# Grouped-query attention and a gated MLP on one core: scores of eight units taken in pairs, and two loads per batch moved

## The chip, the cores and the metric

The kernel runs on one core of one Trainium2 chip. The metric is device time in microseconds (us), the median of several runs, lower is better. The core's engines work side by side: TensorE (PE, matmuls and transposes, its weight loads shown as PEld), VectorE (DVE), ScalarE (ACT), GpSimd (POOL) and SyncE (SP, which here only issues DMAs). They meet through semaphores.

## The reference

Two stages, in a row, for 8 batches of 384 rows:

```python
# attention: q [8,16,384,64], k and v [8,4,384,64]; 4 query heads share one k/v head
scores = (1 / np.sqrt(D)) * np.matmul(q, k.transpose(0, 1, 3, 2))
attn = softmax(scores)                       # over the last axis
x = np.matmul(attn, v) -> [8, 384, 1024]     # the 16 heads side by side
# gated MLP with a spatial gate
h = np.maximum(x @ w_in, 0.0)                # w_in [1024, 1024]
u, v = h[..., :512], h[..., 512:]
v_n = (v - mean(v)) / np.sqrt(var(v) + 1e-06)
v_s = einsum('ts,bsd->btd', w_spatial, v_n) + b_spatial[None, :, None]
out = (u * v_s) @ w_out                      # w_out [512, 1024], float32
```

## The kernel before

**Units.** The attention of a batch is cut into 18 units, counted on through the batches, so that unit 18 is the first of batch one and unit 144 would be the end. Three units (three blocks of 128 keys) make a set: 128 query positions of eight query heads. A batch has six sets; sets 0 and 1 cover the first 128 query positions, and so on. For a unit, `units` (L264 to L287) issues two score matmuls `sc` (L278): each contracts over 64 rows, the two use the two halves of TensorE's rows, and each writes a PSUM bank of 128 x 512. `exp` (L288) has ACT turn each into `aT`. When a set's exps are there, `weigh` (L292) multiplies `aT` by v in 12 matmuls `av` per row half (L298), and DVE divides by the sums: a reciprocal `r` (L311) and a product `x` (L313).

**From x to the MLP.** The MLP wants x transposed (`xt`). In batch zero PE does it (`x_turn`, L324, tile `xps`, copied by DVE at L216). From batch one on a DMA does (`x_send`, L334, issued by SP at L337), one for each 128 query positions, when both of their sets are weighed. q and k are transposed likewise: by PE for the first two batches (`q_turn`, `k_turn`; tiles `qps`, `kps`, copied to `qT`, `kT` by DVE), later by DMA (`q_send`, `k_send`, L256 and L248). The MLP's parts on PE are `pv` (L353, x times the second half of w_in), `pu` (L412, the first half), `psp` (L431, the spatial gate) and `po` (L469, w_out); each ends in an eviction by DVE or ACT: `vr` (L367) with statistics (L379, L380), `uT` (L423), `vs` (L443), `osb` (L216). POOL normalizes (`vn`, L397) and gates (`gT`, L448).

**The order on PE** is written out. A loop over units 0 to 20 (`ALONE = 21`) issues the scores of one unit, then the steps due at that unit (`todo`: transposes, casts, loads), then the weighings due, and then pours matmuls of the MLP, drawn from the generator `gated`, until a budget `spare` is used up: 736 ns for a unit, less 224 for each transpose and 372 for each weighing. From unit 21 on a second loop takes three units (a whole set) at a time: six scores in a row, then fractions of a fixed share of MLP matmuls between the weighings and the due steps.

**PSUM** has eight banks. `bank` gives each new tile the bank that by a planner's estimated release times comes free first; the release times come from fixed costs in `reads`. If the estimate is off, PE waits for the engine that empties the bank.

**Loads.** For batches four to seven a loop (L674 ff.) sets, by units ahead of the batch's first unit `u0`, when loads, casts (POOL) and transposing sends are issued. Loads of k, v and q, the sends and the stores of finished rows all go through SP's one queue in program order, so an instruction that waits there holds back those behind it. `at` appends to the list of a unit; within a group of three units the second loop issues the steps of all three together, behind the late weighings and so behind `x_send`.

Of the kernel before, what the change touches and what calls it, by code (L numbers as in the profile page):

```python
# [17 lines left out]
def kernel(  # L18
# [58 lines left out]
    def bank(shape, dtype, name):  # L77
        i = min(range(8), key=done.__getitem__)
        t = ps.tile(shape, dtype, name=name, tag=f"bank{i}")
        clock[nc.tensor] = max(clock[nc.tensor], done[i])  # L80
        done[i] = 1e12 + clock[nc.tensor]
        taken[name] = i
        return t

    def spend(ns):
        clock[nc.tensor] += ns

    def reads(eng, ns, name=None):
        clock[eng] = max(clock[eng], clock[nc.tensor] + 200.0) + ns
        if name:  # L90
            done[taken.pop(name)] = clock[eng]
# [172 lines left out]
    def units(u, count):  # L264
        b, r = divmod(u, UNITS)
        s, kt0 = divmod(r, NT)
        qt, j = divmod(s, 2)
        kts = range(kt0, kt0 + count)
        if kt0 == 0:
            aTs[b, s] = att.tile([P, NT, 2, G * P], FP16, name=f"aT_{b}_{s}", tag="aT", bufs=3)  # L270
        scs = [
            (kt, hh, bank([P, G * P], FP32, f"sc_{b}_{s}_{hh}_{kt}"))
            for hh in range(2)
            for kt in kts
        ]
        for kt, hh, sc in sorted(scs, key=lambda x: x[:2]):
            rows = slice(hh * D, (hh + 1) * D)
            nc.tensor.matmul(  # L278
                sc,
                kTs[b][rows, j, kt * P : (kt + 1) * P],  # L280
                qTs[b, j][rows, qt].rearrange("p (r i c) -> p i r c", r=G, i=G),
                start=True,
                stop=True,
            )
        spend(count * C512 + 186)
        return [(aTs[b, s][:, kt, hh], sc, f"sc_{b}_{s}_{hh}_{kt}") for kt, hh, sc in scs]

    def exp(a, sc, name):  # L288
        reads(act, 480.0, name)
        act.activation(a, sc, AF.Exp, scale=scale)  # L290

    def weigh(b, s, hh):  # L292
        qt, j = divmod(s, 2)
        aT = aTs[b, s]
        av = bank([P, 512], FP32, f"av_{b}_{s}_{hh}")
        for kt in range(NT):
            for i in range(G):
                nc.tensor.matmul(  # L298
                    av[:, i * (D + 1) : (i + 1) * (D + 1)],
                    aT[:, kt, hh, i * P : (i + 1) * P],  # L300
                    v1[b % 2][:, 2 * j + hh, kt, 0 : D + 1],
                    start=(kt == 0 and i == 0),
                    stop=(kt == NT - 1 and i == G - 1),
                )
        if s == 0 and hh == 0:
            x16s[b] = att.tile([P, NT, DM], FP16, name=f"x16_{b}", tag="x16")
        o = av[:, 0 : G * (D + 1)].rearrange("p (i d) -> p i d", i=G)
        spend(372)
        r = small.tile([P, G, 1], FP32, name=f"r_{b}_{s}_{hh}", tag="r")
        reads(dve, 600.0, f"av_{b}_{s}_{hh}")  # L310
        dve.reciprocal(r, o[:, :, D : D + 1])  # L311
        c = j * 512 + hh * 256
        dve.tensor_tensor(  # L313
            x16s[b][:, qt, c : c + 256].rearrange("p (i d) -> p i d", i=G),
            o[:, :, 0:D],
            r.to_broadcast([P, G, D]),
            ALU.mult,
        )
        measure()
# [243 lines left out]
    def at(n, f, *args):  # L563
        todo.setdefault(n, []).append((f, args))
# [109 lines left out]
    for b in range(4, B):  # L674
        u0 = UNITS * b
        at(u0 - 24, load_k, b)
        at(u0 - 24, load_v, b)
        at(u0 - 22, load_q, b, 0)
        at(u0 - 20, load_q, b, 1)
        at(u0 - 16, cast_k, b, pool)  # L680
        at(u0 - 14, cast_q, b, 0, pool)
        at(u0 - 12, k_send, b)
        at(u0 - 10, q_send, b, 0)
        at(u0 - 10, cast_q, b, 1, pool)
        at(u0 - 8, q_send, b, 1)
        at(u0 - 4, cast_v, b, pool)
# [9 lines left out]
    def pour(n, owed):  # L696
        while owed > 0:
            if n < wait_for[0]:
                return 0.0
            x = next(fill, None)  # L700
            if x is None:
                return 0.0
            if isinstance(x, tuple):
                wait_for[0] = x[1]
            else:
                owed -= x
        return owed

    def turn_x(b, s, n):
        if s % 2 and b:  # L710
            x_send(b, s // 2)

    ALONE = 21
    F = (0.2, 0.3, 0.1, 0.4)
    owed = 0.0
    halves = {}
    for u in range(ALONE):
        for pair in units(u, 1):
            exp(*pair)
        spare = 736  # L720
        for f, args in todo.pop(u, []):
            f(*args)
            spare -= 224 if f in (q_turn, x_turn, k_turn) else 0
        for b, s in ends.pop(u, []):
            halves.setdefault(u, []).append((b, s, 0))
            halves.setdefault(u + (0 if s == 0 else 1), []).append((b, s, 1))
        for h in halves.pop(u, []):
            weigh(*h)
            spare -= 372
            if h[2]:  # L730
                turn_x(*h[:2], u)
        owed = pour(u, min(owed, 0) + spare)
# [64 lines left out]
```

## Time and profile before

| | us |
|---|---|
| median of 3 runs | 239.31 (238.87 to 239.68) |
| the profiled execution, its own time | 239.07 |
| its span, first to last instruction | 237.0 |
| PE busy | 230.4 |
| ACT busy | 169.4 |
| DVE busy | 142.9 |
| POOL busy | 101.4 |

The span is what the profile's times count in; the 2.07 us around it belong to the launch. Ends of matmuls are modelled in the profile, so for PE the differences between starts tell more than durations. Lines named L... are lines of the kernel before. The page's groups show the matmuls of scores with 380 ns each, but two of them run side by side. The waits view lists idle time of an engine over 0.15 us and what ended it; shorter waits of PE are seen only in the time line.

### The profile page before, as it was taken

The page shows a single profiled execution, that of the slowest core. Times are in us where ns is not written, and L with a number is a line of the kernel's source. Part 1 is how long each engine was busy: PE and PEld are TensorE (multiplying, and loading weights), DVE is VectorE, ACT ScalarE, POOL GpSimd, SP SyncE. Part 2 cuts the span into 40 slices and gives each one's busy share as a digit, 9 for nine tenths or more (in the row PEclk, how much of TensorE's full clock was granted, in tenths as well). Part 3 has the DMA queues.
Part 4 walks back from the last instruction along what each step waited for, and adds up shares of the span by engine and source line. Part 5 has one row for each costly group of instructions (what it writes and reads, how often), then busy time and mean ns, then how long its engine had stood idle before and what let it go on. Part 6 is the DMA issues. An engine that isn't in the chain of part 4 may idle for free.

```text
span 237.0 us, 5921 instructions
## 1 busy us (share of the span) xinstructions
PE 230.4 (97%) x2312; PEld 123.3 (52%) x2312; DVE 142.9 (60%) x379; ACT 169.4 (71%) x348; POOL 101.4 (43%) x145
## 2 busy tenths in 40 slices
PE   6999999999999999999999999999999999999993
PEld 6545565645554445555464445555465455545541
DVE  2668775676447674566645577366744767367362
ACT  2999989969897869978697776986597776401211
POOL 3679583551466442275045800566022500460550
PEclk9999999999999999999999999999999999999999
DMA  6999949999999999997998599929912543240147
GB/s 184 290 321 313 278 116 166 167 321 215 297 226 238 332 300 180 354 205 184 169 309 203 182 207 295 272 88 159 253 27 44 114 147 96 48 177 0 66 200 268
DMA packets 67467, 47.47 MB, mean 200 GB/s; under 512 B 48336, under 2 KB 60416, under 8 KB 67440
## 3 DMA queue, kind: packets, MB, share of 16 engines
q1 hardware_dynamic: 62512, 39.86, 67.7%
q0 software_dynamic: 3952, 6.42, 12.1%
q10 hardware_dynamic: 976, 0.82, 1.1%
q8 instruction: 18, 0.29, 0.5%
q14 instruction: 9, 0.07, 0.1%
HBM read 25.95 MB, written 12.58 MB: 163 GB/s over the span
## 4 chain that ended last, share of the span: by engine, by line
PE 79%; DMA 15%; DVE 1%; POOL 1%; SPq 1%; issue 0%
PE pu L412 17%; PE po L469 16%; PE pv L353 15%; PE sc L278 12%; PE av L298 12%; PE psp L431 6%; DMA xt<-x 4%; DMA w_in<-in_moe_w_in_dram 4%; DMA q<-in_q_dram 3%; DMA v_None<-in_v_dram 2%; DMA qT<-q 2%; POOL vn L397 1%; PE qps L238 1%; DVE osb L216 1%; POOL q L204 0%; SPq L256 0%
## 5 line engine op out<-in xcount | busy, mean ns | idle before, releaser
L290 ACT ACTIVATE aT<-sc 128x512 f16<-128x512 f32 x288 | 147.7, 618 | 31.5 <-PE sc L278 30.5
L298 PEld LDWEIGHTS <-aT 128*128 128x128 f16 x1152 | 47.0, 97 | 16.8 <-issue 2.0
L353 PE MATMUL pv<-w_in,xt 128*128 128x512 f16 x192 | 50.9, 380 | 0.4 <-DMA w_in<-in_moe_w_in_dram 0.2
L298 PE MATMUL av<-v,aT 128*128 128x65 f16 x1152 | 50.5, 193 | 0.0
L469 PE MATMUL po<-w_out,gT 128*128 128x512 f16 (+2 forms) x196 | 50.5, 375 | 0.0
L412 PE MATMUL pu<-xt,w_in 128*128 128x384 f16 x256 | 49.9, 326 | 0.0
L397 POOL TENSOR_SCALAR vn<-vr,rstd,nmr 128x512 f16<-128x512 f32 x23 | 17.7, 783 | 69.9 <-DVE nmr L392 48.5
L448 POOL TENSOR_TENSOR gT<-vs,uT 128x384 f16<-128x384 f32 x31 | 32.5, 1059 | 31.9 <-DVE r L311 16.9
L313 DVE TENSOR_TENSOR x<-av,r 128x256 f16<-128x256 f32 x96 | 40.7, 424 | 3.3
L278 PE MATMUL sc<-qT,kT 64*128 64x512 f16 x288 | 42.3, 380 | 0.5 <-DVE qT L216 0.2
L311 DVE RECIPROCAL r<-av 128x4 f32<-128x4 f32 x96 | 17.1, 178 | 40.8 <-PE av L298 40.5
L216 DVE COPY osb<-po 128x512 f32<-128x512 f32 (+1 forms) x39 | 26.6, 683 | 17.3 <-PE po L469 17.2
L412 PEld LDWEIGHTS <-w_in 128*128 128x128 f16 x256 | 22.1, 98 | 17.1 <-issue 5.5
L423 ACT ACTIVATE uT<-pu 128x384 f16<-128x384 f32 x32 | 15.8, 495 | 16.1 <-PE pu L412 16.0
L469 PEld LDWEIGHTS <-gT 128*128 128x128 f16 x196 | 17.4, 98 | 17.3 <-issue 3.3
L353 PEld LDWEIGHTS <-xt 128*128 128x128 f16 x192 | 15.8, 97 | 18.0 <-issue 5.1
L278 PEld LDWEIGHTS <-kT 64*128 64x128 f16 x288 | 11.0, 94 | 25.4 <-issue 13.8
L431 PE MATMUL psp<-wsT,vn 128*128 128x384 f16 x96 | 22.2, 327 | 0.0
L443 DVE TENSOR_TENSOR vs<-psp,bias_bc 128x384 f32<-128x384 f32 x32 | 17.6, 552 | 7.0 <-PE psp L431 6.9
L367 DVE TENSOR_SCALAR vr<-pv 128x512 f32<-128x512 f32 x24 | 16.4, 682 | 8.4 <-PE pv L353 8.3
L201 POOL CAST q<-q 128x768 f16<-128x768 f32 x22 | 17.7, 833 | 7.8 <-PE av L298 3.0
L379 DVE BATCH_NORM_STATS2 stats<-vr 128x6 f32<-128x512 f32 x24 | 16.4, 685 | 0.1
(47 smaller groups left out, 98.0 us busy)
## 6 DMA issues: line engine op xcount, KB each, us to landing
out_dram<-osb SPq DMA_DIRECT2D x21, 512.0 KB, 2.8
q<-in_q_dram SPq DMA_DIRECT2D x10, 768.0 KB, 7.3
v_None<-in_v_dram SPq DMA_DIRECT2D x6, 384.0 KB, 4.5
w_in<-in_moe_w_in_dram POOLq DMA_DIRECT2D x4, 512.0 KB, 10.4
k_None<-in_k_dram SPq DMA_DIRECT2D x5, 384.0 KB, 3.9
q<-in_q_dram POOLq DMA_DIRECT2D x2, 768.0 KB, 8.7
out_dram<-osb SPq DMA_DIRECT2D x5, 256.0 KB, 2.3
w_out<-in_moe_w_out_dram POOLq DMA_DIRECT2D x2, 512.0 KB, 9.4
```

The lines of the kernel that those rows point to most:

```text
L201: eng.tensor_copy(t16[:, :, :, hh, :], src[:, hh])
L216: (act.copy if eng is act else dve.tensor_copy)(o, i)
L278: nc.tensor.matmul(sc, kTs[b][rows, j, kt * P : (kt + 1) * P], qTs[b, j][rows, qt].rearrange("p (r i c) -> p i r c", r=G, i=G), start=True ...
L290: act.activation(a, sc, AF.Exp, scale=scale)
L298: nc.tensor.matmul(av[:, i * (D + 1) : (i + 1) * (D + 1)], aT[:, kt, hh, i * P : (i + 1) * P], v1[b % 2][:, 2 * j + hh, kt, 0 : D + 1], st ...
L313: dve.tensor_tensor(x16s[b][:, qt, c : c + 256].rearrange("p (i d) -> p i d", i=G), o[:, :, 0:D], r.to_broadcast([P, G, D]), ALU.mult,)
L353: nc.tensor.matmul(pv, xts[b][:, kt, st * P : (st + 1) * P], w_in16[:, kt, DH:DFF], start=(kt == 0), stop=(kt == NK - 1),)
L397: (dve if b == 0 and st == 1 else pool).tensor_scalar(vn, v_r.pop((b, st)), rstd[:, st : st + 1], nmr[:, st : st + 1], op0=ALU.mult, op1=A ...
L412: nc.tensor.matmul(pu[:, 0:S], w_in16[:, kt, m * P : (m + 1) * P], xts[b][:, kt, :], start=(kt == 0), stop=(kt == NK - 1),)
L431: nc.tensor.matmul(psp[:, 0:S], v_n[b, st][:, m * P : (m + 1) * P], wsT16[:, st, :], start=(st == 0), stop=(st == NT - 1),)
L448: pool.tensor_tensor(gT, vs, uT, ALU.mult)
L469: nc.tensor.matmul(po[:, 0:width], gTs[b][:, m, tt * P : (tt + 1) * P], w_out16[:, m, c0 : c0 + width], start=(m == 0), stop=(m == NM - 1),)
```

## The change

Units 13 to 20 are taken two at a time: at units 13, 15, 17 and 19 the loop issues the scores and exps of that unit and the next, and at 14, 16, 18 and 20 none. The steps and weighings due at each unit stay with it. The budget for MLP matmuls becomes 600 ns at the units with scores and 870 at those without.

For batches four to seven the second q load moves from 20 to 17 units ahead of the batch, and the v load from 24 to 15 units ahead. In the loop of three units at a time this puts the q load behind the last `x_send` of the batch two in front, and the v load one group of three later.

```diff
@@ -674,9 +674,9 @@
     for b in range(4, B):
         u0 = UNITS * b
         at(u0 - 24, load_k, b)
-        at(u0 - 24, load_v, b)
         at(u0 - 22, load_q, b, 0)
-        at(u0 - 20, load_q, b, 1)
+        at(u0 - 17, load_q, b, 1)
+        at(u0 - 15, load_v, b)
         at(u0 - 16, cast_k, b, pool)
         at(u0 - 14, cast_q, b, 0, pool)
         at(u0 - 12, k_send, b)
@@ -714,10 +714,15 @@
     F = (0.2, 0.3, 0.1, 0.4)
     owed = 0.0
     halves = {}
+    TWO = 13
     for u in range(ALONE):
-        for pair in units(u, 1):
-            exp(*pair)
-        spare = 736
+        if u < TWO or (u - TWO) % 2 == 0:
+            pairs = units(u, 1)
+            if u >= TWO and u + 1 < ALONE:
+                pairs += units(u + 1, 1)
+            for pair in pairs:
+                exp(*pair)
+        spare = 736 if u < TWO else (600 if (u - TWO) % 2 == 0 else 870)
         for f, args in todo.pop(u, []):
             f(*args)
             spare -= 224 if f in (q_turn, x_turn, k_turn) else 0
```

## The prediction

> **What bounds the kernel now.** I read the page's first part (busy time by engine), then the waits, then the time line of PE around the edited units, DVE's beside it, and last the chain that ended last, at its DMA links.
>
> ```profile
> PE 230.4 (97%) x2312; PEld 123.3 (52%) x2312; DVE 142.9 (60%) x379; ACT 169.4 (71%) x348; POOL 101.4 (43%) x145
> ```
>
> PE is busy for 97% of the span, at a granted clock of 0.998. So time is won only by taking work or a short wait out of PE's stream; what another engine saves counts only where PE waits for it. The edited units run between 17 and 32 us; that stretch, and under it PE's rows of it, with a group of three units from later in the run:
>
> ```profile
> 17.00:32.00 15.00, 14.93 (x206) 8.33 (x205) 11.82 (x37) 13.87 (x28) 11.06 (x20) 1.00 1.02 278
> ```
>
> ```profile
> 17.24 0.59 PE L353 MATMUL pv<-w_in,xt 128*128 128x512 f16 x2
> 17.77 0.39 PE L278 MATMUL sc<-qT,kT 64*128 64x512 f16 x2
> ...
> 18.86 0.39 PE L278 MATMUL sc<-qT,kT 64*128 64x512 f16 x2
> 19.18 0.54 PE L298 MATMUL av<-v,aT 128*128 128x65 f16 x12
> ...
> 72.03 0.82 PE L278 MATMUL sc<-qT,kT 64*128 64x512 f16 x6
> 72.78 0.60 PE L469 MATMUL po<-w_out,gT 128*128 128x512 f16 x2
> ```
>
> The columns of the first are PE, PEld, DVE, ACT, POOL (us busy of 15.00): PE 14.93, ACT 13.87, DVE 11.82. All three are nearly full here, unlike in the whole span. Of the time line read the differences between starts. A pair of scores (x2, the two row halves run side by side) holds PE from 18.86 to 19.18, 0.32 us; two pv ahead of one hold it from 17.24 to 17.77, 0.53, where two of them inside a run take 0.43. So one unit alone costs 0.10 + 0.32 = 0.42 us. Three units together go from 72.03 to 72.78: 0.75, with the 0.10 ahead 0.85, so a further unit in the same group costs (0.85 - 0.42) / 2 = 0.21. A score group thus pays about 0.20 us for being a group.
>
> DVE, which empties most of PSUM, in the same stretch:
>
> ```profile
> 20.34 0.68 DVE L379 BATCH_NORM_STATS2 stats<-vr 128x6 f32<-128x512 f32 x1
> 21.06 0.18 DVE L380 BATCH_NORM_AGGREGATE mv<-stats 128x2 f32<-128x6 f32 x1
> 21.16 0.15 DVE L311 RECIPROCAL r<-av 128x4 f32<-128x4 f32 x1
> 21.34 0.42 DVE L313 TENSOR_TENSOR x<-av,r 128x256 f16<-128x256 f32 x1
> ...
> 31.05 0.41 DVE L216 COPY qT<-qps 128x512 f16<-128x512 f16 x1
> 31.38 0.42 DVE L216 COPY xt<-xps 128x512 f16<-128x512 f16 x1
> ```
>
> The x of 21.34 ends at 21.77; PE's x turn that reads it starts at 21.81. The xt copy ends at 31.80, and the fourth score of the group at 31.19, whose bank it frees, starts at 31.85 (0.43 behind the third; 0.01 is usual). So PE's next losses lie on DVE.
>
> From the chain, the links where PE meets a DMA after the start:
>
> ```profile
> 50.15 4.90 DMA qT<-q
> 55.09 1.15 PE sc L278 x6
> ...
> 75.15 10.13 DMA xt<-x
> 85.33 0.60 PE pv L353 x2
> ```
>
> These two landings (at 55.05 and 85.28) are met by PE without slack: whatever PE gains before them is lost there unless the landing comes earlier too.
>
> **Edit 1, scores two units in a row.** The instructions stay the same; the order on PE changes. Of the eight groups of two scores of units 13 to 20, four go into the group before them: 4 x 0.20 = 0.81 us less on PE (0.203 unrounded). This is on the path, as PE has no idle time to hide it in. The pours change from 8 x 736 = 5888 ns to 4 x (600 + 870) = 5880: the matmuls that fill PE between scores are the same, except that one pv (0.215) goes ahead of unit 21 instead of behind it. From unit 24 on the order on PE is the old one.
>
> What it adds is pressure on DVE and on the banks. The DVE instructions are the same and in the same order, so I walked them beside PE from unit 13 (18.86) on, with the steps of the rows: av to its end 0.54 and 0.04 to the next engine, r to x 0.21, x to the next 0.34, a copy 0.33, vr 0.60, stats 0.72, mv 0.10. Six places where PE then waits:
>
> - x turn of x columns 4 to 7 behind units 15 and 16: PE is there at 21.81 as before, but the first av of set 3 now stands behind four scores and ends at 19.94 instead of 19.72, so r starts 19.98, x 20.20, stats 20.54, r 21.36, x 21.56 to 21.98. PE waits 0.19, where it waited 0.
> - the pv and the x turn behind the next two pairs, each for an xt or x just copied: 0.05 and 0.05.
> - the group of units 21 to 23: its second score takes the bank of the last pv, whose copy vr runs from 26.99 to 27.67: 0.14 lost (before 0.10: start 27.87, end 28.72, against 0.75).
> - x turn of the last set of batch one: its bank is that of the av before, whose x ends 30.10; PE is there at 29.85: 0.29 (before the av behind it lost 0.08).
> - the group of units 24 to 26: its fourth score waits for the xt copy, by the walk to 31.32 (before 31.80): 0.31 lost there. Before 0.43 there and 0.09 ahead of it.
>
> New waits 0.19 + 0.05 + 0.05 + 0.14 + 0.29 + 0.31 = 1.03, old ones 0.10 + 0.08 + 0.09 + 0.43 = 0.70. So 0.33 of the 0.81 is given back and 0.48 stays: pv behind unit 26 at 31.89 instead of 32.37. Bounds: 0.81 if DVE's waits are no longer than before (and 0.70 more could in principle go with them, though DVE's own 11.82 of 15.00 us leave little), 0 if DVE's chain sets the pace. I take the walk, as its steps are rows of this very stretch.
>
> ACT: an exp follows the one before at 0.49 us, four take 1.95; two units in the walk take 2.1 to 2.3 on PE, so ACT waits 0.15 to 0.3 per pair and does not bind. The nearest bank that an exp must free for a score (unit 18's, by the exp of unit 16) is free 0.3 us ahead.
>
> A rule that speaks against edit 1: the Trainium skill, TensorEngine Tiling (Array Packing), Performance Considerations, says that tiling makes TensorE faster but not the emptying of PSUM, which may become the bottleneck. By that rule taken fully edit 1 would bring nothing and the time be 238.9. The trace agrees in part: the 31.80 to 31.85 handover is such a wait, and DVE still has 3.18 us free.
>
> At 55.09 the lead of 0.48 meets the qT landing. Without that landing PE would have started those scores at 54.94; but the fourth of them starts at 55.65, when vr has emptied its bank, and the pv behind at 56.29, when x (55.72 + 0.42) has emptied another. These follow PE and come 0.48 earlier. Were the landing not to move at all, scores from 55.09 would give the pv at 55.83 to 55.85, which still keeps 0.44 to 0.46. And it should move: its chain goes back through q loads and sends in SP's order to the x send at 34.26, released by an x of DVE at 34.23, which comes earlier with PE. Later landings have more slack: qT of batch three 70.97 for scores at 72.03, q of batch two's second set 58.33 for 59.65.
>
> **Edit 2, the loads.** On SP's queue, for batch four, k, v, q0, q1, out, x send become k, q0, out, x send, q1, out, v, x send of batch three. The x send of 75.15 takes 10.13 us: ahead of it 384 + 384 + 768 + 768 + 512 KB stand in the same queue, landing at 76.2, 77.3, 80.5, 83.1 and 84.5, then xt at 85.28. Without v (1.15 us) and q1 (2.56) it lands near 85.28 - 3.71 = 81.6. PE wants it at 85.18 (84.43 + 0.75), so 0.14 of waiting goes and, more to the point, the lead of edit 1 survives: it would need the landing at 84.7. SP issues nothing more or less, and no load gains a wait of length: the buffers of q1 and v have been read 20 us earlier. What moves behind: q1 lands near 84 to 85 (before 83.1), v near 87, behind the next out (before 77.3). POOL casts q1 at 83.20 and v at 84.75 now, and next has vn at 93.25; so POOL waits some 2 us longer and has 6 us to spare. Ahead of the x send of batch three (82.90) SP's queue holds the same transfers as before in another order, so that send and kT and qT behind it should land as now: qT of batch four at 92.58 and 94.00, wanted at 96.70 and 100.78. In batches five to seven PE has no wait for a DMA now (no PE idle over 0.15 us from 80 to 200), and x sends have 5 us and more, so there the edit is worth 0.
>
> **Sum**, against the profiled execution's own 239.07 (span 237.0 and 2.07 around it): -0.81 + 0.33 - 0.14 = -0.62, so 238.45. That execution is 0.24 below the median 239.31 and inside the runs (238.87 to 239.68).
>
> **The rivals.**
> 1. The waits on DVE do not grow: the whole 0.81 + 0.14 comes, 238.1. For it: the six waits are each under 0.3 us and built from handovers of 0.04; against it: DVE has 3.2 us free in 15, in pieces.
> 2. The lead is lost, to a chain on DVE that sets the pace or to transfers that keep their times: 0.14 is left, 239.07 - 0.14 = 238.9. For it: DVE is at 79% of that stretch (11.82 of 15.00); against: the walk.
> 3. Slower: scores four in a row want four banks at once. If the second unit's scores find theirs still to be read by an exp, PE stands for one exp (0.49) in each of the four pairs, 1.95, against the 0.81 saved: 239.07 + 1.95 - 0.81 - 0.14 = 240.1. It decides from about 0.24 us per pair on. The walk has 0.3 us of slack there, so exps would have to come 0.5 us later than their rows.
> 4. Slower by the loads: v or q1 of batch four lands so late that POOL's vn starts behind 93.25, or qT after 96.70. From there each us late costs a us; it takes 4 to 6 us more than worked out above. I count it with rival 3.
>
> **Chances and range.** Forecast 0.46, rival 1 0.24, rival 2 0.16, rivals 3 and 4 0.14. The forecast's own range is 238.2 to 238.75 (0.25 either way, the sum of six waits of 0.05 to 0.3). For 8 in 10: down to rival 1 less the part of old waits that might go, 237.8, and up past rival 2 to 239.4, which leaves out most of rivals 3 and 4. From no change one can tell about 0.3%, 0.72 us: below 238.35 lie rival 1 and a third of the forecast, 0.40; within it the rest of it and rival 2, 0.46; slower 0.14.
>
> **What would show it.** PE's score groups of x4 at about 18.9, 21.1, 23.2 and 25.3 us; pv behind unit 26 near 31.9; DVE as what ends PE's short waits at 22.0, 27.7, 30.1 and 31.4; xt of batch two landing near 82 and PE's scores near 84 without the wait behind. Wrong would be: exps as releaser of scores in that stretch, the lead at 56 us smaller than at 32, or a POOL or PE wait on q, v or qT of batch four.

## The result, and the profile after

The changed kernel's median is 238.94 us over 21 runs (237.84 to 239.68). The kernel before, run beside it and with the three first runs counted in, had 240.65 over 21 (238.53 to 244.4). The ratio is of the fast runs alone: it leaves out three of before (242.53 to 244.4 us, more than 1.5% above its fastest), and the other 18 have a median of 239.68, 0.74 us above the changed kernel's. It is 0.9952, with a 95% interval of 0.993 to 0.9973: faster by half a percent, where the likeliest case of the prediction was a gain of 0.26%, inside the 0.3% that one can tell from no change. The profiled execution took 238.38 us with a span of 236.4 (before 239.07 and 237.0); the prediction's sum was 238.45.

The first part of the page of the changed kernel, and its stretch from 17 to 32 us (columns PE, PEld, DVE, ACT, POOL in us busy):

```profile
PE 230.1 (97%) x2312; PEld 123.6 (52%) x2312; DVE 142.7 (60%) x379; ACT 169.5 (72%) x348; POOL 101.5 (43%) x145
```

```profile
17.00:32.00 15.00, 14.85 (x210) 8.66 (x209) 12.39 (x38) 14.25 (x29) 12.32 (x23) 1.00 1.04 287
```

The shares over the span say nothing of the change. In the stretch the same 15 us hold more work: ACT 14.25 for 13.87, DVE 12.39 for 11.82. PE's time line of the pairs, start and duration ahead:

```profile
18.98 0.61 PE L278 MATMUL sc<-qT,kT 64*128 64x512 f16 x4
19.52 0.54 PE L298 MATMUL av<-v,aT 128*128 128x65 f16 x12
...
21.22 0.61 PE L278 MATMUL sc<-qT,kT 64*128 64x512 f16 x4
21.76 0.34 PE L224 MATMUL kps<-ident,k 128*128 128x128 f16 x3
21.93 0.49 PE L330 MATMUL xps<-ident,x 128*128 128x128 f16 x4
22.26 0.39 PE L238 MATMUL qps<-ident,q 128*128 128x128 f16 x4
22.48 0.53 PE L298 MATMUL av<-v,aT 128*128 128x65 f16 x12
22.94 0.39 PE L353 MATMUL pv<-w_in,xt 128*128 128x512 f16 x1
23.27 0.60 PE L278 MATMUL sc<-qT,kT 64*128 64x512 f16 x4
...
25.32 0.61 PE L278 MATMUL sc<-qT,kT 64*128 64x512 f16 x4
...
29.63 0.39 PE L238 MATMUL qps<-ident,q 128*128 128x128 f16 x4
30.17 0.40 PE L330 MATMUL xps<-ident,x 128*128 128x128 f16 x4
...
30.86 1.10 PE L278 MATMUL sc<-qT,kT 64*128 64x512 f16 x6
31.89 0.82 PE L353 MATMUL pv<-w_in,xt 128*128 128x512 f16 x3
```

Two units go from 18.98 to 19.52, 0.54 us, with 0.10 ahead 0.64, against 2 x 0.42 before: the 0.20 per group is there. The four groups start within 0.12 us of the places predicted (18.9, 21.1, 23.2, 25.3). The x turn of 21.93 to 22.26 takes 0.33 instead of 0.23: a wait for x of 0.10, which the prediction put at 0.19. Other waits are read in the same way. The av of 22.48 is followed by a pv after 0.46 us, where 0.37 is usual, because the pv reads an xt copied just before (0.09). From qps at 29.63 to xps at 30.17 it is 0.54 instead of 0.22, a wait for the bank of an av, whose x ends at 30.11 (0.31). The six scores of 30.86 take 1.03 instead of 0.75 (0.28), and those of unit 21, at 27.56, take 0.90 (0.14). The pv behind unit 26 starts at 31.89, the time predicted, though this execution reached unit 13 0.12 us later than that of before.

At the landing of xt of batch two, SP's queue and then PE in the changed kernel, and last PE in the kernel before:

```profile
71.95 0.53 SPq L112 DMA_DIRECT2D k_None<-in_k_dram  x1
72.53 0.54 SPq L122 DMA_DIRECT2D q<-in_q_dram  x1
73.18 0.41 SPq L484 DMA_DIRECT2D out_dram<-osb  x1
74.18 1.99 SPq L337 DMA_TRANSPOSE xt<-x  x1
```

```profile
83.92 0.82 PE L278 MATMUL sc<-qT,kT 64*128 64x512 f16 x6
84.68 0.60 PE L353 MATMUL pv<-w_in,xt 128*128 128x512 f16 x2
```

```profile
84.43 0.82 PE L278 MATMUL sc<-qT,kT 64*128 64x512 f16 x6
85.33 0.60 PE L353 MATMUL pv<-w_in,xt 128*128 128x512 f16 x2
```

The x send is issued at 74.18 and its data land 8.3 us later, at 82.46 (before: issued 75.15, landed 85.28). The scores of 83.92 are followed after 0.76 us by the pv that reads xt, where before it was 0.90: the 0.14 us of waiting are gone.

What can't be seen in one pair of traces is how much of the difference is the edits'. So for every traced execution I took the starts of PE's scores and read the run in stretches. Unit n to unit m means from the first score of n to the first score of m.

| execution | unit 11 starts | unit 13 | 13 to 27 | 63 to 66 | 66 to the end | xt of batch two landed | span |
|---|---|---|---|---|---|---|---|
| before | 16.55 | 18.86 | 17.06 | 4.10 | 148.46 | 85.28 | 237.00 |
| changed | 16.67 | 18.98 | 16.46 | 3.97 | 148.47 | 82.46 | 236.36 |

The executions of the experiments are added below. From unit 66 on all agree to 0.05 us. Before unit 13, which neither edit reaches, the changed kernel's execution was 0.12 us later than that of before, so behind the start the two differ by 0.64 + 0.12 = 0.76 us: 0.60 between units 13 and 27, 0.13 at the landing, 0.04 between units 36 and 39. The last belongs to that one execution of before: in two others, traced later, before took the same 4.18 us there as the changed kernel.

### The profile page after: what moved, and what is told of

The parts are those of the page before. It is cut to its first block, busy times and chain, and to the rows that moved or that the text cites. A ratio compares the mean times of both kernels' runs of the same rounds, so it can differ in the third digit from the quotient of the medians.

```text
span 236.4 us, 5917 instructions
## 1 busy us (share of the span) xinstructions
PE 230.1 (97%) x2312; PEld 123.6 (52%) x2312; DVE 142.7 (60%) x379; ACT 169.5 (72%) x348; POOL 101.5 (43%) x145
## 4 chain that ended last, share of the span: by engine, by line
PE 93%; DVE 2%; DMA 2%; issue 0%; ACTq 0%; ACT 0%
PE pu L412 18%; PE pv L353 18%; PE po L469 18%; PE sc L278 15%; PE av L298 15%; PE psp L431 7%; DMA q<-in_q_dram 2%; PE qps L238 1%; PE xps L330 1%; DVE x L313 1%; DVE osb L216 1%; DVE qT L216 0%; DVE q L206 0%; DVE r L311 0%; DVE vr L367 0%
## 5 line engine op out<-in xcount | busy, mean ns | idle before, releaser
L278 PE MATMUL sc<-qT,kT 64*128 64x512 f16 x288 | 41.6, 380 | 0.4 <-DVE qT L216 0.2
L278 PEld LDWEIGHTS <-kT 64*128 64x128 f16 x288 | 10.9, 94 | 23.7 <-issue 12.1
```

The lines of the kernel that those rows point to most:

```text
L278: nc.tensor.matmul(sc, kTs[b][rows, j, kt * P : (kt + 1) * P], qTs[b, j][rows, qt].rearrange("p (r i c) -> p i r c", r=G, i=G), start=True ...
```

## The experiments

My theory after the result: the gain is 0.60 us of PE time from the pairs, kept by the earlier landing; what the medians show beyond that is scatter of the start. The rivals: the landing moves by itself and the loads need not be moved; or the loads are the main thing, as they spare executions with late transfers; or DVE sets the pace and more grouping would bring nothing.

**Each edit alone, both again, and before against itself.** The first kernel has only the pairs:

```diff
-        at(u0 - 17, load_q, b, 1)
-        at(u0 - 15, load_v, b)
+        at(u0 - 24, load_v, b)
+        at(u0 - 20, load_q, b, 1)
```

> Only the scores of units 13 to 20 in pairs; the loads stay where they were. Theory A (the gain is PE time, 0.5 to 0.6 us up to unit 27 as the profile after shows, and what the landing of xt of batch two at 85 us lets through): PE's scores of unit 27 about 0.5 us earlier than before, and from unit 66 on only as much as that landing comes earlier; in the profile after, the sends just ahead of the loads came 0.39 earlier, so some 0.4 us stay and PE's wait ahead of the first pv of that block grows from 0.14 to about 0.2; ratio about 0.998. Rival B (the landing is set by the transfers alone): the lead at unit 66 is 0, ratio 1.000. Rival C (the median's 1.15 us come from executions in which transfers land late, and the moved loads are what removes them): the times of this kernel scatter like those of before, 238.5 to 244.

The second has only the loads moved, and the loop over the units as before:

```diff
-    TWO = 13
...
-        spare = 736 if u < TWO else (600 if (u - TWO) % 2 == 0 else 870)
+        for pair in units(u, 1):
+            exp(*pair)
+        spare = 736
```

> Only the second q load and the v load of batches four to seven moved; the scores stay in single units. Theory A: 0.14 us, the wait for xt at 85 us alone, ratio about 0.9994, and the same scatter as before. Rival C: the scatter goes (all within 1.5 us, as after), the median falls by 0.6 us or more, ratio 0.997 or less. Rival D (the scatter has to do with the start, the landings of the first loads, and with neither edit): the scatter stays as it is in before.

> The changed kernel once more, on this chip. All theories: ratio within 0.993 to 0.9975. A and D: its times scatter as widely as those of the kernel before beside it; C: they stay within 2 us while those of before reach over more.

> The kernel before against itself: ratio 1.000 within its interval, which tells how far two sets of runs of one kernel lie apart. Its profile is a second execution of before: under C a slow one shows PE waiting longer for a DMA near 55 or 85 us; under D all of the difference stands before unit 13.

Against 35 runs of before on the same chip (median 239.34):

| kernel | median of 12 | ratio (95%) |
|---|---|---|
| pairs only | 239.06 | 0.9981 (0.9951 to 1.0011) |
| loads only | 238.86 | 0.9993 (0.9962 to 1.0024) |
| both | 238.89 | 0.9982 (0.9959 to 1.0005) |
| before | 239.55 | 1.0013 (0.9983 to 1.0043) |

The medians can't tell these apart: the kernel before lies 0.13% from itself, and the changed kernel's 0.9952 has become 0.9982, outside the 0.993 to 0.9975 expected. The rival that the times of before scatter because of the loads found no support either: loads only scattered from 238.13 to 240.9, pairs only from 237.88 to 242.25, before from 238.25 to 241.95. That both again stayed at 238.31 to 240.16 is no proof, as a later series gave it 237.72 to 240.83.

The first traced execution of pairs only took 242.25 us, the longest of its twelve. Units 13 to 27 took 16.46 us in it too; where it lost time is said below the table of all executions.

**The pairs alone once more, only v moved, threes, and pairs from unit 11 on.**

> The pairs of scores with the loads where they were, one look. Unit 13 to unit 27 takes 16.46 us as in the changed kernel (before 17.06). Theory A (the landing of xt of batch two comes as much earlier as the sends ahead of it, some 0.4 us): it lands near 84.9, PE waits 0.2 to 0.3 for it, and 0.3 to 0.4 of the 0.6 stay. Rival B (the landing is set by the queue's backlog alone; in two executions of before it came at 85.3 and 85.1 though PE was 0.9 us apart): it lands at 85.1 to 85.3, PE waits 0.5 to 0.7, unit 63 to 66 takes 4.4 to 4.7 instead of 3.97, and nothing stays.

Only v moved is the changed kernel with the second q load back in its place:

```diff
-        at(u0 - 17, load_q, b, 1)
+        at(u0 - 20, load_q, b, 1)
```

> The pairs of scores, and of the loads only v moved; the second q load stays ahead of the x send. By the sizes of the queue's steps (v 1.15 us) xt of batch two lands near 84.0 instead of 85.2, and PE, which wants it at 84.6 plus what the start is late, does not wait: unit 63 to 66 takes 3.97. If the order ahead of the x send did not set the landing, it would stay at 85.2 and unit 63 to 66 take 4.4 or more.

```diff
-    TWO = 13
+    TWO = 12
-        if u < TWO or (u - TWO) % 2 == 0:
+        if u < TWO or (u - TWO) % 3 == 0:
             pairs = units(u, 1)
-            if u >= TWO and u + 1 < ALONE:
-                pairs += units(u + 1, 1)
+            if u >= TWO:
+                pairs += units(u + 1, 1) + units(u + 2, 1)
...
-        spare = 736 if u < TWO else (600 if (u - TWO) % 2 == 0 else 870)
+        spare = 736 if u < TWO else (464 if (u - TWO) % 3 == 0 else 872)
```

> Both edits, but units 12 to 20 in three groups of three instead of one single and four pairs: two groups fewer. If PE's group cost alone decides: unit 12 to unit 27 takes 17.55 - 2 x 0.20 = 17.15 us (before 18.15, changed kernel 17.55). If DVE's chain sets the pace: 17.5 or more, with longer waits of PE for DVE's copies. If exps hold the banks of a group's last scores (six exps take 2.9 us): scores wait for ACT and it takes 17.6 to 18.2.

```diff
-    TWO = 13
+    TWO = 11
...
-        measure()
+        if b or hh:
+            measure()
```

> Both edits, pairs from unit 11 on (one group fewer), and the statistics of batch zero only behind the second weighing of a set, so that they no longer stand ahead of the x that the x turn reads. Unit 11 to unit 27: before 19.37 us, changed kernel 18.77. If PE's group cost and the one x turn's wait of 0.1 decide: 18.77 - 0.20 - 0.10 = 18.47. If DVE's later chain takes it back at unit 24: 18.6 to 18.77.

Pairs only: unit 13 to 27 took 16.46, as said. Its start was very late (unit 13 at 21.06), xt landed at 86.98, PE waited 0.27 (63 to 66 took 4.24). The wait is the one theory A gave, but with PE 2.2 us later than in before at unit 13 the place of the landing can't be compared; one more execution was needed.

Only v moved: xt landed at 84.74, later than the 84.0 expected, with PE itself 0.6 us late; 63 to 66 took 3.96, no wait. One load out of the way is enough, with 0.5 us to spare (84.52 + 0.75 = 85.27 is when PE wants it).

Threes: unit 12 to 27 took 18.24 us, where the changed kernel takes 17.55 and before 18.15. Two groups fewer cost 0.69 us instead of gaining 0.40. PE's time line of the threes kernel:

```profile
18.00 0.82 PE L278 MATMUL sc<-qT,kT 64*128 64x512 f16 x6
18.76 0.40 PE L238 MATMUL qps<-ident,q 128*128 128x128 f16 x4
19.07 0.38 PE L330 MATMUL xps<-ident,x 128*128 128x128 f16 x4
19.67 0.52 PE L298 MATMUL av<-v,aT 128*128 128x65 f16 x12 [0.21 <-DVE qT L216]
...
25.89 0.33 PE L224 MATMUL kps<-ident,k 128*128 128x128 f16 x3
26.48 0.38 PE L330 MATMUL xps<-ident,x 128*128 128x128 f16 x4 [0.27 <-DVE qT L216]
```

The six scores themselves run through (18.00 to 18.76, as later in the run), so no exp holds a bank. What waits are the transposes and av behind them, for copies of DVE: the brackets name them. The transposes of three units come in one bunch, and PE stands until a bank is emptied. DVE itself was not full here: it had stood idle for 0.87 and 0.88 us, waiting for the transposes, just ahead of the two copies that the brackets name (19.19 and 26.01). Whether another choice of banks would spare these waits was not tried.

Pairs from unit 11 on: unit 11 to 27 took 18.90 us for 18.77 in the changed kernel, more than either case of the expectation. Units 11 to 13 cost 2.51 for 2.31, as there a later x turn waits for its x; units 13 to 21 took 8.52 for 8.58, which is all that the later statistics brought. Neither variant beats the changed kernel. PE also lost 0.88 us between units 36 and 39 in this execution, at a place that the prediction does not name:

```profile
49.92 1.03 PE L470 MATMUL po<-w_out,gT 128*128 128x512 f16 x4
51.67 0.52 PE L298 MATMUL av<-v,aT 128*128 128x65 f16 x12 [0.72 <-ACT aT L290]
```

```profile
49.56 1.17 POOL L204 CAST q<-q 128x512 f16<-128x512 f32 x2 [2.06 <-DMA q<-in_q_dram]
50.79 0.83 POOL L189 CAST v<-v_None 128x768 f16<-128x768 f32 x1
```

Both fences are of that kernel, PE and then POOL. The bracket on PE names ACT, but POOL's cast of v ends at 50.79 + 0.83 = 51.62 and the av starts at 51.67: it waited for v of batch two, whose cast stands behind one of q that waited for its load. In the traced execution of before the same cast ended at 51.00 and the av started at 51.05. An execution in which that load comes late can lose time there.

**A third series of the four kernels.**

> Before once more. Theory A (the edits' worth is 0.60 us between unit 13 and unit 27, plus what the xt landing costs an execution between units 63 and 66; the rest of the scatter is the start, up to unit 11, which no edit touches): unit 13 to 27 takes 17.06, unit 63 to 66 between 3.96 and 5.1, all other stretches from unit 66 on equal to 0.02 us; ratio 1.000 within 0.003. Rival B (something else in the executions of before is slower, which one trace did not show): a stretch outside of these differs.

> Pairs without the moved loads. Theory A: unit 13 to 27 takes 16.46; unit 63 to 66 more than 3.96, by 0.2 us or more, since PE comes earlier to a landing that has not; ratio 0.997 to 0.999.

> Moved loads without pairs. Theory A: unit 13 to 27 takes 17.06, unit 63 to 66 takes 3.96 to 3.98; ratio 0.9985 to 1.000.

> Both edits. Theory A: unit 13 to 27 takes 16.46 and unit 63 to 66 takes 3.96 to 3.98; ratio 0.996 to 0.998, lower than that of either edit alone. Were the first series' 0.9952 the edits' own worth, it would come again below 0.996.

Against 34 runs of before (median 239.48): before 1.000 (0.9972 to 1.0028), pairs only 0.9967 (0.9937 to 0.9996), loads only 0.998 (0.9953 to 1.0007), both 0.9965 (0.9937 to 0.9993). The first series' 0.9952 did not come again. Pairs only and loads only came out somewhat better than expected (0.997 to 0.999 and 0.9985 to 1.000). By the ratios pairs only is as good as both, in this series and in the one before. Its trace shows that it can lose its gain. Pairs only, third series: the chain that ended last, and then PE's time line.

```profile
75.01 10.32 DMA xt<-x
85.33 0.05 issue
85.38 0.60 PE pv L353 x2
```

```profile
83.72 0.82 PE L278 MATMUL sc<-qT,kT 64*128 64x512 f16 x6
85.38 0.60 PE L353 MATMUL pv<-w_in,xt 128*128 128x512 f16 x2 [0.84 <-DMA xt<-x]
```

And both edits, third series:

```profile
83.58 0.82 PE L278 MATMUL sc<-qT,kT 64*128 64x512 f16 x6
84.33 0.60 PE L353 MATMUL pv<-w_in,xt 128*128 128x512 f16 x2
```

PE came 0.7 us earlier than in before (83.72 for 84.43), xt landed at 85.33 for 85.28, and PE stood 0.91 us, where before had stood 0.14. So in this execution the lead of 0.7 is gone, and from unit 66 on this execution is level with that of before (88.59 for 88.54). With the loads moved, PE goes on after 0.75 us.

All executions read in the same way (the last two columns are differences, so that the start drops out):

| execution | unit 11 starts | 13 to 27 | 63 to 66 | xt landed | span | unit 13 to the end |
|---|---|---|---|---|---|---|
| before | 16.55 | 17.06 | 4.10 | 85.28 | 237.00 | 218.14 |
| before again | 17.46 | 17.06 | 3.96 | 85.11 | 237.72 | 217.95 |
| before, third | 17.00 | 17.06 | 4.06 | 85.65 | 237.36 | 218.05 |
| loads only | 16.53 | 17.06 | 3.96 | 83.37 | 236.79 | 217.94 |
| loads only, third | 16.42 | 17.06 | 3.96 | 82.97 | 236.68 | 217.94 |
| pairs only, second | 18.74 | 16.46 | 4.24 | 86.98 | 238.70 | 217.64 |
| pairs only, third | 16.48 | 16.46 | 4.87 | 85.33 | 237.04 | 218.25 |
| changed | 16.67 | 16.46 | 3.97 | 82.46 | 236.36 | 217.38 |
| both again | 17.13 | 16.46 | 3.96 | 83.33 | 236.77 | 217.33 |
| both, third | 16.34 | 16.46 | 3.96 | 81.23 | 235.97 | 217.32 |
| only v moved | 17.27 | 16.46 | 3.96 | 84.74 | 236.95 | 217.37 |

So, shown by undoing each part: the pairs are worth 0.60 us up to unit 27 in every execution that has them, and with the moved loads PE does not wait for this xt (five of five at 3.96 or 3.97; with only v moved too). That the loads bring the landing forward shows best when the start is taken out. From the issue of k, the first of these loads (72.34 in before, 71.95 in the changed kernel), to the landing of xt it took 12.8 to 13.1 us in the five executions with the loads where they were, 12.1 with v moved and 10.5 to 11.3 in the five with both moved. In the two executions of pairs only, the gain of the pairs was lost in part (second: 217.64) or whole (third: 218.25).

How often that happens is not shown. Nine of the twelve runs of pairs only in the third series were shorter than the traced one (239.10 us), though its start is among the earliest of the table; and the ratios of pairs only (0.9981 and 0.9967) are those of both edits (0.9982 and 0.9965). So what the moved loads add to the pairs over many runs was too small for these series to tell. Mean from unit 13 on: before 218.05 (three), both 217.34 (three): the two edits together are worth 0.71 us, 0.30%.

What the times of these eleven executions show beyond that lies ahead of unit 13. Unit 11 started between 16.34 and 18.74 us in these executions, 2.4 us apart, three times the edits' worth. PE's waits there differ from one execution to the next: 1.5 us for a cast of q by POOL in before again, 1.1 us for a landing of w_in in both again and 0.8 us for the same in before, third. Time can be lost behind the start too: the first traced execution of pairs only lost 1.36 us between units 36 and 39, where pairs from unit 11 on lost 0.88, and 1.13 us between units 63 and 66.

Three series of the changed kernel against before gave 0.9952, 0.9982 and 0.9965, on average 0.9966 or 0.8 us, in line with 0.71. Why so many runs of before were long in the first series (eight of the 18 behind its ratio took 240.65 us or more, against 4 of 34 and 6 of 32 in the others) is open: the one trace of before from it has an early start and a time of 239.07, so that the long runs began late is a guess.

## Why the prediction was right or wrong

- **Score groups, 4 x 0.20 us.** Right: 0.54 us for a pair behind the switch in, groups where they were put.
- **The give-back of 0.33 us to DVE.** Right in kind and place, too large: 0.81 less the measured 0.60 is 0.21. The walk's time of unit 13 to 27 was 16.58, measured 16.46. The six waits of the walk, 0.19, 0.05, 0.05, 0.14, 0.29 and 0.31, were in the changed kernel's execution 0.10, 0.09, none, 0.14, 0.31 and 0.28: 0.92 for 1.03. The largest miss is the first x turn: the walk had all four transposes wait for the second x of the set, but the first two read the first x and ran at once; only the third waited. Units 21 to 24 took 3.30 for 3.27 and units 24 to 27 took 4.58 for 4.61.
- **ACT does not bind.** Right in pairs and even in threes: no score waited for an exp. "DVE, which empties most of PSUM" holds only beside the scores: in the stretch ACT's 28 exps empty a bank of scores each, while DVE empties 23 other tiles.
- **The rule against edit 1.** The Trainium skill, TensorEngine Tiling (Array Packing), Performance Considerations, says that the copy out of PSUM may become the bottleneck after a fourfold speed-up of TensorE. In pairs the trace bears this out for 0.21 of 0.81 us, by which PE's waits for DVE grew. In threes, 0.69 us slower than pairs, the waits that the trace names end with DVE's copies, with DVE idle in between.
- **qT at 55 us.** Right that nothing is lost there. Both, third, even waited 0.2 us for that qT and had it back one group later (units 39 to 45 took 7.06 us, as in the changed kernel's first trace). The prediction did not see that the cast of v of batch two, 0.05 us ahead of its av, has no slack at all; in the eleven executions of the table it cost 0.04 us once, in the first of before.
- **Edit 2.** The mechanism was right: xt landed at 82.46 (81.6 predicted), q1 and v later without cost. The term was mis-sized. 0.14 us was the wait in one execution of before; others had 0 and 0.10. The step said that the lead of edit 1 would need an earlier landing and that the edit gives it: pairs only shows that PE can wait 0.9 us there without it, far more than the 0.14 entered, and, in its other execution, 0.27.
- **The sum.** 0.62 predicted, 0.71 measured from unit 13 on (0.76 in the two first traces). The term that was mis-sized is the give-back to DVE, 0.33 for a measured 0.21. The wait at the landing, entered at 0.14, was 0.13 in these two traces and 0.08 on the mean of three of before. That 238.45 us stands so near to the 238.38 of the profiled execution is in part luck: behind the start it gained 0.14 more than predicted, but it started 0.12 late.
- **The call.** The step that failed is "within it the rest of it and rival 2, 0.46", that a gain of this size would most likely look like no change. With 0.62 so near to the border of 0.72, an error of 0.1 in the give-back brings the case to the border, and the chance for "faster" should have been the larger. The base was one execution that lay inside three runs of before (238.87 to 239.68). The 18 runs behind the ratio reached from 238.53 to 241.94, and nothing in the sum stands for that. The first series' 0.48%, 1.15 us, is 0.4 more than the traces show for the edits. No term of the sum explains it, and its cause stays open. That the measured change lay clear of no change owes something to that scatter: the second series, at 0.9982 (0.9959 to 1.0005), did not tell it from none.
- **The slower rivals** did not come: neither exps nor the loads of batch four held PE.

## What to carry to other kernels

Where PE is full and another engine nearly, cut PE's fixed costs in small steps: two units per group kept three quarters of the 0.81 us, three per group lost more than they saved, with PE waiting for copies that came in a bunch. A gain ahead of a transfer is only as good as that transfer's landing: check each landing that PE meets later with less slack than the gain, and move what stands ahead of it in its queue. And where the start of an execution scatters by more than an edit is worth, compare traces by stretches that begin behind the start. Here a few executions then told 0.1 us, where the intervals of a dozen runs or two were 0.5 to 0.7 us to either side.

## What the runs showed that I had not expected

The landing of xt of batch two follows its queue rather than PE. In three executions of before and one of pairs only, PE reached unit 63 at 84.43, 85.31, 84.85 and 83.72, a spread of 1.6 us, and xt landed at 85.28, 85.11, 85.65 and 85.33, within 0.54. In the other execution of pairs only it landed at 86.98; there k, the first of the 2.8 MB of loads and stores ahead of it in the queue, was issued later as well, at 73.99 for 72.09 to 72.86. In all five the landing came 12.8 to 13.1 us behind that issue.

The start varies without any edit: up to unit 11 all these programs but one do the same, with the same data, and unit 11 began anywhere between 16.3 and 18.7 us, while stretches behind it in which PE meets no late transfer repeat to 0.05 us (units 13 to 27 of one kernel to 0.01).
